# Attention and two MoE layers on one core: the first weight splits pinned behind exponentials, an early activation, and the first weight loads queued behind rows of q and k

## The chip, the cores and the metric

One core of one Trainium2 chip runs the whole kernel. The metric is the time of one execution on the device in microseconds (us), as the median of several runs.

## What is computed

Random-feature attention over 4 batches, 8 heads, 576 positions of 64 elements, and then two feed-forward layers over its 2304 rows of 512. The weights of both layers come in float64; everything else is float32.

```python
def phi(x):                                  # q and k, both scaled by 64 ** -0.25
    h = x @ omega.T - sum(x * x) / 2         # 128 features
    return exp(h - max(h)) / sqrt(128)
kv, z = k_p.T @ v, sum(k_p)                  # per head
attn = (q_p @ kv) / (q_p @ z + 1e-6)
x = attn.transpose(0, 2, 1, 3).reshape(2304, 512)
x = ((x @ w_a) * (x @ w_b)) @ w_out          # d_ff 1536: 12 slabs f of 128
out = relu(x @ w_in) ** 2 @ w_out2           # d_ff 2048: 16 slabs
```

## The kernel before

Matmuls of the two layers run as three products of a high and a low part, so each float64 weight slab is loaded raw as pairs of 32-bit words and split on chip: `load` (L125) issues the DMAs on SP into one of two raw buffers, `split` (L142) makes the two parts with three ScalarE instructions (L151, L152, L163) and five of VectorE (L155, L159, L164, L168, L172). `load_split` (L184) does the load at once and puts the split on a list; `step()` (L196), called once for each step of the work around it, counts the list down, and a split is written into the program three steps after its load. The split tiles `a` and `p` exist once, so splits run one after the other.

The program is given as a sequence; a scheduler then orders the instructions of each engine by their place in it and by when it expects their inputs, and adds the semaphores. An engine runs its own list in order.

At the start, `prologue` (L233) transposes `omega` on TensorE and makes `OMS`, `OMZ` and `OM` of it on ScalarE (L247 to L251). `start_lanes` (L805) then does batch 0: `k_lane(0, (0,))`, and for each pair of heads p the steps of q, merged in turns with those of the next k pair. A k pair (`k_steps`, L407) loads its rows (`Side`, L310) and V, transposes them (`t1_main`, L330), copies them to `S` (L333), projects and exponentiates in two halves (`phi_wide`, L278: matmuls L285, a minimum L289, four exponentials L291), and multiplies with V (L423). A q pair (`q_steps`, L463) does the same for its rows up to the exponentials, transposes the features (L474), multiplies (L481), divides and turns the result into `x_all` (L492 to L499). The sequence makes 54 steps, 0 to 53: k pair 0 with its tail 0 to 9, q pair 0 with k pair 1 10 to 20, q pair 1 with k pair 2 21 to 36, q pair 2 with k pair 3 37 to 47, q pair 3 48 to 53. The exponentials of k pair 0 stand at steps 4 and 6, of k pair 1 at 15 and 17, of k pair 2 at 30 and 33; rows of q pair 0 and k pair 1 are loaded at 10 and 11, of q pair 1 and k pair 2 at 21 and 22.

Between those steps the loop at L887 takes the first weights from `get_first` (L873): the first slabs of `w_a` and `w_b` (key `("a", 0)`), then `w_out`'s first (`("o", 0)`), and so on, one call of it at each step S0, S0 + SD, and so on. With S0 = 1, SD = 8 the loads stand at steps 1, 17, 25, 41 and 49. After the lanes the MoE passes begin (`a_units`, L599): `proj` (L610) multiplies x with `w_a` and `w_b`, `outs` (L635) with `w_out`, and the rest of attention runs in their gaps.

Of the kernel before, what the change touches and what calls it, by code (L numbers as in the profile page):

```python
# [8 lines left out]
F32 = mybir.dt.float32  # L9
# [4 lines left out]
ACTF = mybir.ActivationFunctionType  # L14
# [21 lines left out]
def f32(ap):  # L36
    return ap.bitcast(F32)


def i32(ap):  # L40
    return ap.bitcast(I32)
# [3 lines left out]
def kernel(  # L45
# [13 lines left out]
    nc = tc.nc  # L59
# [65 lines left out]
    def load(*parts):  # L125


        raw = top["raw"].tile([128, 2, 512, 2], I32, tag="raw", name="raw")
        for x, (w, f, rows) in enumerate(parts):
            t = raw[:, x]  # L130
            if rows:
                nc.sync.dma_start(
                    out=t.rearrange("p f w -> p (f w)"), in_=w[f * 128:(f + 1) * 128, :]
                )
            else:
                nc.sync.dma_start(
                    out=t.rearrange("p (k f) w -> p k (f w)", k=KC),
                    in_=w[:, f * 256:(f + 1) * 256].rearrange("(k p) f -> p k f", p=128),
                )
        return raw[:, 0:len(parts)]  # L140

    def split(raw, t):  # L142

        n = raw.shape[1]
        up = raw[:, :, :, 1]
        u = raw[:, :, :, 0]
        a = top["cut"].tile([128, 2, 512], F32, tag="a", name="a")[:, 0:n]
        p = top["cut"].tile([128, 2, 512], F32, tag="p", name="p")[:, 0:n]  # L150
        nc.scalar.activation(out=a, in_=f32(up), func=ACTF.Copy, scale=WORD_SCALE)  # L151
        nc.scalar.activation(  # L152
            out=u, in_=raw.bitcast(U16)[:, :, :, 1], func=ACTF.Copy, scale=2.0 ** 7,
        )
        nc.vector.tensor_scalar(  # L155
            out=i32(p), in0=i32(a), scalar1=3, scalar2=0x7FFFF000,
            op0=ALU.logical_shift_left, op1=ALU.bitwise_and,
        )
        nc.vector.scalar_tensor_tensor(  # L159
            out=i32(p), in0=i32(a), scalar=-0x80000000, in1=i32(p),  # L160
            op0=ALU.bitwise_and, op1=ALU.bitwise_or,
        )
        nc.scalar.copy(out=t[:, :, 0, :], in_=p)  # L163
        nc.vector.scalar_tensor_tensor(  # L164
            out=u.bitcast(U32), in0=up.bitcast(U32), scalar=23, in1=u.bitcast(U32),
            op0=ALU.logical_shift_left, op1=ALU.bitwise_or,
        )
        nc.vector.tensor_scalar(  # L168
            out=i32(a), in0=i32(p), scalar1=-0x00800000, scalar2=None,
            op0=ALU.bitwise_and,  # L170
        )
        nc.vector.scalar_tensor_tensor(  # L172
            out=t[:, :, 1, :], in0=u.bitcast(U32), scalar=2.0 ** -43, in1=a,
            op0=ALU.mult, op1=ALU.mult,
        )
# [4 lines left out]
    def split_next():  # L180
        _, _, fn = waiting.pop(0)
        fn()

    def load_split(key, parts, t, steps, then=None):  # L184
        while len(waiting) > 1:
            split_next()
        raw = load(*parts)

        def fn():
            split(raw, t)  # L190
            if then:
                then()

        waiting.append([steps, key, fn])
# [11 lines left out]
    def get_pair(key, steps, pool, tag, *parts):  # L206
        t = pool.tile([128, 2, 2, 512], F32R, tag=tag, name=tag)
        load_split(key, parts, t, steps)
        return t[:, 0], t[:, 1]
# [4 lines left out]
    ap2 = actx.enter_context(tc.tile_pool(name="ap2", bufs=2))  # L214
# [11 lines left out]
    state = {"at": [0, 1, 2, 3, 4, 5, 6, 7], "n": 0}  # L226

    def at_bank(shape, name):
        i = state["at"][state["n"] % len(state["at"])]
        state["n"] += 1  # L230
        return bank(i, shape, name)

    def prologue():  # L233
        make_identity(nc, ident)
        nc.sync.dma_start(out=om[:, 0, :], in_=omega)
        nc.sync.dma_start(out=om[:, 1, :], in_=omega)


        nc.vector.memset(V, 1.0)
        nc.vector.memset(VT, 1.0)  # L240
        nc.vector.memset(VT[64:128, :, :, 0, :], 0.0)
        nc.vector.memset(VT[0:64, :, :, 1, :], 0.0)
        nc.vector.memset(OMZ, 0.0)
        ps = at_bank([128, M], "ps_om")
        nc.tensor.transpose(ps, om.rearrange("p a d -> p (a d)"), ident)

        nc.scalar.mul(out=OMS, in_=ps, mul=-SCALE)  # L247
        for x in range(2):
            r = slice(64 * x, 64 * x + 64)
            nc.scalar.mul(out=OMZ[r, x, :], in_=ps[r], mul=-SCALE)  # L250
        nc.scalar.copy(out=OM[:, 0, :], in_=OMS)  # L251
        nc.vector.tensor_tensor(out=OM[:, 1, :], in0=OMS, in1=f32(OM[:, 0, :]), op=ALU.subtract)
# [25 lines left out]
    def phi_wide(rows, dst):  # L278


        n = 2 * len(rows)
        nm = ap2.tile([128, n], F32, tag="nm", name="nm", bufs=4)
        ps = at_bank([128, n, M], "ps_p")
        for x, s in enumerate(rows):
            nc.tensor.matmul(  # L285
                ps[:, 2 * x:2 * x + 2].rearrange("p h m -> p (h m)"), lhsT=s,
                rhs=OMZ.rearrange("p h m -> p (h m)"), start=True, stop=True,
            )
        nc.vector.tensor_reduce(out=nm, in_=ps, axis=AXX, op=ALU.min)  # L289
        for x in range(n):  # L290
            nc.scalar.activation(  # L291
                out=dst[:, x, :], in_=ps[:, x, :], func=ACTF.Exp, scale=-1.0,
                bias=nm[:, x:x + 1],
            )

    class Side:
# [4 lines left out]
        def __init__(self, src, nm, b, p, chunks):  # L301
            self.nm = nm
            self.wide = (nm, b) in WIDE or (nm, b) == ("q", 1) and 0 in chunks
            self.main = chunks
            nj = len(chunks)
            h = slice(2 * p, 2 * p + 2)
            j0 = chunks[0]
            self.nat = ap1.tile([128, 2, nj, D], F32, tag=f"{nm}n", name=f"{nm}n", bufs=2)
            v_ = src[b, h, 0:SM, :].rearrange("h (p j) d -> p h (j d)", j=4)
            nc.sync.dma_start(  # L310
                out=self.nat.rearrange("p h j d -> p h (j d)"),
                in_=v_[:, :, j0 * D:(j0 + nj) * D],
            )
# [59 lines left out]
    def kt_steps(b, g):  # L373
# [13 lines left out]
        yield  # L387
        kp = ap2.tile([128, 2, M], F32, tag="qp", name="kpt", bufs=2)
        phi_wide([st], kp)
        yield  # L390

# [409 lines left out]


    prologue()

    def start_lanes():  # L805
# [67 lines left out]
    def get_first():  # L873
        for f in range(W_FIRST):
            get_w(f)
            yield
            yield
            get_wo(f)
            yield
        for f in range(W_FIRST, 3):  # L880
            get_wo(f)
            yield

    lanes, n = start_lanes()
    first = get_first()
    S0, SD = 1, 8
    for i, _ in enumerate(lanes):  # L887
        step()
        if i >= S0 and (i - S0) % SD == 0:
# [105 lines left out]
```

## Time and profile before

| | us |
|---|---|
| median of 3 runs | 1050.73 |
| lowest and highest | 1049.35, 1052.2 |
| the profiled execution | 1052.61 |
| its span, first to last instruction | 1050.8 |
| TensorE busy in the span | 1024.0 |

The profile is of one execution. Its rows give for each engine when it worked, how long it was idle and what ended the idle time. PE is TensorE's matmuls, PEld its weight loads, which run beside them; ACT is ScalarE, DVE VectorE, POOL GpSimd, SP the engine that issues most DMAs. Ends of matmuls are modelled, so a busy PE isn't PE at its peak.

### The profile page before, as it was taken

How to read it: one execution, taken by the hardware profiler on the slowest of the kernel's cores; microseconds unless marked ns; L12 is line 12 of the kernel's file. 1: busy time of each engine (PE TensorE's matmuls, PEld its weight loads, DVE VectorE, ACT ScalarE, POOL GpSimd, SP SyncE). 2: the span in 40 equal slices, each digit the busy share in tenths (PEclk: the TensorE clock that was granted, in tenths of full speed). 3: DMA queues.
4: the chain of work that ended last, by engine and by line, in shares of the span. 5: the costliest groups of instructions: out<-in, count | busy, mean ns of one | idle time of the engine just before them, and what ended most of it. 6: DMA issues, size and time to landing. Idle time of an engine off the chain costs nothing.

```text
span 1050.8 us, 14948 instructions
## 1 busy us (share of the span) xinstructions
PE 1024.0 (97%) x5641; PEld 873.6 (83%) x5641; DVE 526.8 (50%) x1274; ACT 471.2 (45%) x1079; POOL 28.9 (3%) x54
## 2 busy tenths in 40 slices
PE   4899999999999999999999999999999999999998
PEld 3789989999988877788888888788788888888887
DVE  4788885665654445444337987722222322322222
ACT  4887757554455443333326665522322322322232
POOL 3100101000000000000000000000000000000000
PEclk9999999999999999999999999999999999999999
DMA  6846864663432211312227664300200200100010
GB/s 166 242 148 205 267 233 120 210 209 95 142 105 80 63 46 56 95 62 70 66 87 264 230 220 174 107 1 0 81 1 1 71 1 1 51 1 1 0 41 21
DMA packets 83144, 105.90 MB, mean 101 GB/s; under 512 B 26240, under 2 KB 65152, under 8 KB 83072
## 3 DMA queue, kind: packets, MB, share of 16 engines
q1 hardware_dynamic: 81536, 103.37, 30.7%
q0 software_dynamic: 1536, 1.58, 0.5%
q8 instruction: 45, 0.74, 0.3%
q14 instruction: 27, 0.22, 0.1%
HBM read 87.62 MB, written 17.30 MB: 100 GB/s over the span
## 4 chain that ended last, share of the span: by engine, by line
PE 88%; DVE 4%; DMA 3%; ACT 3%; issue 1%; SPq 1%; ACTq 0%; DVEq 0%
PE abw L610 19%; PE o L764 19%; PE ph L777 18%; PE y L635 12%; PE ab L610 7%; PE ps_n L481 3%; PE ps_p L285 2%; PE ps_kv L423 2%; PE ps_p L351 2%; PE ps_qt L474 1%; DMA raw<-in_moe_w_out_dram 1%; PE ps_t L330 1%; DMA qn<-in_q_dram 1%; DVE p L159 1%; PE ps_x L492 1%
## 5 line engine op out<-in xcount | busy, mean ns | idle before, releaser
L635 PE MATMUL y<-gs,wo 128*128 128x256 f32 (+1 forms) x864 | 177.2, 345 | 0.0
L764 PE MATMUL o<-w,ss 128*128 128x512 f32 x702 | 170.9, 390 | 1.4 <-ACT ss L786 1.4
L777 PE MATMUL ph<-yx,w 128*128 128x512 f32 (+1 forms) x780 | 169.8, 368 | 0.0
L777 PEld LDWEIGHTS ph<-yx,w 128*128 128x128 f32 x780 | 137.4, 188 | 25.3
L785 DVE TENSOR_TENSOR r<-r 128x512 f32<-128x512 f32 (+1 forms) x80 | 51.1, 639 | 209.8 <-ACT r L784 209.8
L764 PEld LDWEIGHTS o<-w,ss 128*128 128x128 f32 x702 | 130.5, 188 | 29.7 <-ACT ss L786 2.2
L635 PEld LDWEIGHTS y<-gs,wo 128*128 128x128 f32 x864 | 136.6, 190 | 15.2
L610 PE MATMUL abw<-x_all,w 128*128 128x512 f32 x576 | 146.6, 398 | 0.0
L784 ACT ACTIVATE r<-ph 128x512 f32<-128x512 f32 (+1 forms) x80 | 44.5, 556 | 208.4 <-PE ph L777 208.2
L610 PE MATMUL ab<-x_all,w 128*128 128x256 f32 x864 | 132.9, 295 | 0.3 <-DVE x_all L549 0.2
L610 PEld LDWEIGHTS abw<-x_all,w 128*128 128x128 f32 x576 | 105.5, 189 | 19.2
L610 PEld LDWEIGHTS ab<-x_all,w 128*128 128x128 f32 x864 | 115.0, 193 | 1.5 <-DVE x_all L549 0.5
L787 DVE TENSOR_TENSOR ss<-r,ss 128x512 fp32r<-128x512 f32 (+1 forms) x80 | 51.1, 639 | 46.6 <-ACT ss L786 40.0
L610 PE MATMUL abw<-x_mid,w 128*128 128x512 f32 x288 | 73.1, 400 | 0.0
L786 ACT CAST ss<-r 128x512 fp32r<-128x512 f32 (+1 forms) x80 | 46.2, 577 | 51.5 <-DVE r L785 51.5
L610 PEld LDWEIGHTS abw<-x_mid,w 128*128 128x128 f32 x288 | 52.1, 189 | 9.8
L358 DVE CUSTOM_DVE_ANT_0 c<-ps_p,c 128x128 f32<-128x128 f32 x152 | 37.8, 287 | 32.5 <-ACT c L356 32.0
L701 ACT CAST gs<-a_s 128x256 fp32r<-128x256 f32 (+1 forms) x96 | 40.6, 433 | 28.3 <-DVE a_s L700 28.1
L164 DVE SCALAR_TENSOR_TENSOR raw<-raw 128x1024 uint32<-128x1024 uint32 (+1 forms) x40 | 42.5, 1062 | 13.4 <-ACT raw L152 13.3
L152 ACT ACTIVATE raw<-raw 128x1024 int32<-128x1024 uint16 (+1 forms) x40 | 40.8, 1020 | 11.4 <-DMA raw<-in_moe_w_out_dram 9.3
L702 DVE TENSOR_TENSOR gs<-a_s,gs 128x256 fp32r<-128x256 f32 (+1 forms) x96 | 42.8, 454 | 5.3 <-ACT gs L701 4.2
L151 ACT ACTIVATE a<-raw 128x1024 f32<-128x1024 f32 (+1 forms) x40 | 40.6, 1014 | 10.9 <-DMA raw<-in_moe_w_out_dram 5.6
(109 smaller groups left out, 1212.9 us busy)
## 6 DMA issues: line engine op xcount, KB each, us to landing
wo<-wo_d SPq DMA_DIRECT2D x60, 512.0 KB, 3.5
raw<-in_moe_w_out_dram SPq DMA_DIRECT2D x28, 512.0 KB, 4.8
raw<-in_moe_w_in_dram SPq DMA_DIRECT2D x16, 512.0 KB, 3.9
raw<-in_moe_w_a_dram SPq DMA_DIRECT2D x12, 512.0 KB, 4.8
raw<-in_moe_w_b_dram SPq DMA_DIRECT2D x12, 512.0 KB, 6.1
wo_d<-wo SPq DMA_DIRECT2D x12, 512.0 KB, 3.4
kn<-in_k_dram SPq DMA_DIRECT2D x16, 256.0 KB, 3.5
V<-in_v_dram SPq DMA_DIRECT2D x16, 256.0 KB, 3.4
```

Source lines behind the costliest of these rows:

```text
L151: nc.scalar.activation(out=a, in_=f32(up), func=ACTF.Copy, scale=WORD_SCALE)
L152: nc.scalar.activation(out=u, in_=raw.bitcast(U16)[:, :, :, 1], func=ACTF.Copy, scale=2.0 ** 7,)
L164: nc.vector.scalar_tensor_tensor(out=u.bitcast(U32), in0=up.bitcast(U32), scalar=23, in1=u.bitcast(U32), op0=ALU.logical_shift_left, op1=A ...
L610: nc.tensor.matmul(ps, lhsT=wv[:, s_, kc, :], rhs=x[..., kc, m_, :], start=(kc == 0 and (s_, m_) == TERMS[0]), stop=(kc == KC - 1 and (s_, ...
L635: nc.tensor.matmul(y_part(pi, f, c), lhsT=wo[pi, f][:, s_, c * 128:(c + 1) * 128], rhs=g[:, m_, :],  start=(f == f0 and (wide or c % 2 == ...
L702: nc.vector.tensor_tensor(out=g[:, 1, c], in0=a_s, in1=f32(g[:, 0, c]), op=ALU.subtract)
L764: nc.tensor.matmul(op[t], lhsT=s_t[f][:, s_, t * 128:(t + 1) * 128], rhs=wo2[f][:, m_, :], start=(f == 0 and (s_, m_) == TERMS[0]), stop=( ...
L777: nc.tensor.matmul(ps, lhsT=wv[:, s_, kc, :], rhs=y[:, kc, m_, :], start=(kc == 0 and (s_, m_) == TERMS[0]), stop=(kc == KC - 1 and (s_, m ...
L784: nc.scalar.activation(out=r, in_=ps, func=ACTF.Relu, scale=1.0 / W_SCALE)
L785: nc.vector.tensor_tensor(out=r, in0=r, in1=r, op=ALU.mult)
L786: nc.scalar.copy(out=s_t[f][:, 0, :], in_=r)
L787: nc.vector.tensor_tensor(out=s_t[f][:, 1, :], in0=r, in1=f32(s_t[f][:, 0, :]), op=ALU.subtract)
```

## The change

An Exp of a column of zeros is put at the head of the prologue. `Side` and `phi_wide` record the last row load and the last exponential that they have written. For the keys `("a", 0)` and `("o", 0)` the raw load is queued, on SP, behind the row load recorded last, and the split's ScalarE instructions behind the exponential recorded last: `issue_after` orders what the block writes on that instruction's own engine behind it. S0 becomes 16 and SD 6, which puts the loads at steps 16, 28, 34, 46 and 52.

```diff
-        raw = load(*parts)
+        if key in (("a", 0), ("o", 0)):
+            with tc.issue_after(state["row"].ins):
+                raw = load(*parts)
+        else:
+            raw = load(*parts)
 
         def fn():
-            split(raw, t)
+            if key in (("a", 0), ("o", 0)):
+                with tc.issue_after(state["exp"].ins):
+                    split(raw, t)
+            else:
+                split(raw, t)
...
     def prologue():
+        warm = ap2.tile([128, 1], F32, tag="den", name="warm", bufs=3)
+        nc.vector.memset(warm, 0.0)
+        nc.scalar.activation(out=warm, in_=warm, func=ACTF.Exp)
         make_identity(nc, ident)
...
         for x in range(n):
-            nc.scalar.activation(
+            state["exp"] = nc.scalar.activation(
                 out=dst[:, x, :], in_=ps[:, x, :], func=ACTF.Exp, scale=-1.0,
...
-            nc.sync.dma_start(
+            state["row"] = nc.sync.dma_start(
                 out=self.nat.rearrange("p h j d -> p h (j d)"),
...
-    S0, SD = 1, 8
+    S0, SD = 16, 6
```

## Rows read from the trace of the kernel before

**Rows 1.** The page, first part: busy us (share of the span) and instructions.

```profile
PE 1024.0 (97%) x5641; PEld 873.6 (83%) x5641; DVE 526.8 (50%) x1274; ACT 471.2 (45%) x1079; POOL 28.9 (3%) x54
```

**Rows 2.** Stages: length, busy PE, PEld, DVE, ACT, POOL, granted clock, DMA share, GB/s.

```profile
0.00:15.00 15.00, 1.86 (x7) 1.20 (x8) 2.50 (x6) 3.10 (x6) 7.79 (x18) 1.00 0.80 218
15.00:25.00 10.00, 9.76 (x48) 8.20 (x49) 7.81 (x12) 8.38 (x24) 0.00 (x0) 1.00 0.34 96
25.00:60.00 35.00, 30.66 (x207) 26.01 (x206) 28.59 (x56) 31.74 (x87) 4.72 (x8) 1.00 0.75 227
60.00:140.00 80.00, 79.78 (x611) 75.55 (x611) 68.70 (x147) 59.74 (x143) 9.41 (x16) 1.00 0.67 211
```

**Rows 3.** Waits, 0 to 62 us: us in total, times, longest.

```profile
PE ps_t L330 <- ACT OMZ L250: 8.7, 1, 8.7
ACT a L151 <- DMA raw<-in_moe_w_b_dram: 1.3, 1, 1.3
```

**Rows 4.** Timeline, 0 to 30 us: start, us, engine, line, operation.

```profile
3.22 0.45 PE L245 MATMUL ps_om<-ident,om 128*128 128x128 f32 x1 [3.22 <-DMA om<-in_omega_dram]
4.90 1.11 PE L330 MATMUL ps_t<-ident,kn 128*128 128x128 f32 x4 [1.24 <-DMA kn<-in_k_dram]
...
11.85 1.28 ACT L151 ACT_TABLE_LOAD   x1 [11.85 <-DMA raw<-in_moe_w_b_dram]
13.14 1.12 ACT L151 ACTIVATE a<-raw 128x1024 f32<-128x1024 f32 x1
14.16 0.27 ACT L247 ACTIVATE OMS<-ps_om 128x128 f32<-128x128 f32 x1
...
15.21 0.59 ACT L333 COPY S<-ps_t 128x512 f32<-128x512 f32 x1
...
26.95 1.22 ACT L291 ACTIVATE kp<-ps_p,nm 128x128 f32<-128x128 f32 x4
```

**Rows 5.** SP's issues (timeline), and DMA issues of 0 to 5 us: median to landing.

```profile
4.27 0.50 SPq L310 DMA_DIRECT2D qn<-in_q_dram  x1
4.82 0.92 SPq L310 DMA_DIRECT2D kn<-in_k_dram  x1
...
qn<-in_q_dram SPq DMA_DIRECT2D x1, 128.0 KB, 8.7
kn<-in_k_dram SPq DMA_DIRECT2D x1, 256.0 KB, 9.3
...
kn<-in_k_dram SPq DMA_DIRECT2D x1, 256.0 KB, 3.2
V<-in_v_dram SPq DMA_DIRECT2D x1, 256.0 KB, 4.8
```

**Rows 6.** Groups of ScalarE, 0 to 30 us: busy us, mean ns, idle before.

```profile
L152 ACT ACTIVATE raw<-raw 128x1024 int32<-128x1024 uint16 (+1 forms) x2 | 1.8, 920 | 0.0
L151 ACT ACTIVATE a<-raw 128x1024 f32<-128x1024 f32 (+1 forms) x2 | 1.8, 909 | 0.0
L163 ACT CAST w<-p 128x1024 fp32r<-128x1024 f32 x1 | 1.1, 1050 | 0.0
L163 ACT CAST wo<-p 128x512 fp32r<-128x512 f32 x1 | 0.7, 719 | 0.0
```

**Rows 7.** Last split steps (timeline), and L610's matmuls in two stretches.

```profile
20.30 1.22 DVE L172 SCALAR_TENSOR_TENSOR w<-raw,a 128x1024 fp32r<-128x1024 uint32 x1
67.20 1.23 DVE L172 SCALAR_TENSOR_TENSOR w<-raw,a 128x1024 fp32r<-128x1024 uint32 x1
...
46.00:68.00 22.00, 9.10 (x56) 1.00 0.76 230
68.00:70.00 2.00, 2.00 (x18) 1.00 0.26 60
```

**Rows 8.** Groups of PE, forms apart, 0 to 20 us, then 20 to 26.

```profile
L285 PE MATMUL ps_p<-OMZ,S 128*128 128x256 f32 x8 | 3.8, 651 | 0.2 <-ACT S L333 0.2
...
L285 PE MATMUL ps_p<-OMZ,S 128*128 128x256 f32 x12 | 3.7, 393 | 0.0
```

## The prediction

> **What bounds the kernel now.** I read the page's busy totals first [rows 1]: TensorE is busy 1024.0 of 1050.8 us, so no edit here can save more than the 26.8 us in which it is idle, and only where the idle time lies matters. The stages [rows 2] say where: from 0 to 15 us PE is busy 1.86 us (13.1 idle), from 15 to 60 us 40.42 of 45 (4.6 idle) and from 60 to 140 us 79.78 of 80. The change touches the beginning alone, so the question is what ends the waits there. The waits name it: the longest one of PE, 8.7 us, is the transpose of q behind `OMZ` [rows 3]. The rows in order of time [rows 4] show why `OMZ` is late. Omega's transpose ends at 3.22 + 0.45 = 3.67 us, and the transposes of the first k pair start at 4.90 and end near 6.0. But ScalarE's first instruction is the first weight split (L151), which waits until 11.85 us for `w_b`; its table load (1.28 us) and its own 1.12 us follow, and `OMS` and `OMZ`, ready to run at 3.67, stand behind it until 14.16 us. The k slab's copy `S` follows at 15.21 us. One instruction issued too early on an in-order engine holds attention back by some 10 us.
>
> There is a second wait under the first. q's first rows are issued at 4.27 us behind both halves of the first weights and land 8.7 us later, at 13.0; the second k pair's, issued at 4.82, land at 14.1 [rows 5]. PE has the transposes of q ahead of the projections of k, so with ScalarE free alone PE would have stood until 13.0 anyway. The two edits need each other.
>
> **The change part by part.** *The early activation* adds a memset of one column, an Exp of one column and moves the table load ahead. The table load was 1.28 us behind the DMA wait, inside the stall, so it isn't added to the gain of the stall. The one-column Exp isn't in the trace; its bound above is a 128x128 one, 1.22 us for four, so 0.3, and the memset's is the same 0.3. Both and the table load are done when they start by 3.67 - 1.28 - 0.6 = 1.8 us, before ScalarE has its first real work, and nothing but the memset stands before them. Counted at nothing; without that cover they would cost up to 1.9.
>
> *The pin of the splits.* I count steps in the lane loop. S0 = 16 loads the first weights at step 16 and, three steps on, traces their split at step 19; the exponentials recorded last by then are the second half of k pair 1 (step 17), the second pair and not the first. w_out's first split is loaded at step 28, traced at 31, pinned behind the first half of k pair 2 (step 30). In the trace of before the k pair 1 exponentials end at 26.95 + 1.22 = 28.2 us [rows 4]. ScalarE is therefore free at 3.67: `OMS`, `OMZ`, `OM` (1.05 us, from 14.16 to `S` at 15.21) run until 4.7, and `S` can start when the k transposes end, at 6.05 instead of 15.21: 9.15 us earlier.
>
> *The loads behind the rows.* SP issues the two weight halves behind q's first rows and k pair 1's, so these take the issue slots at 2.9 and 3.4 us. What they then need is bounded by the nearest rows: k pair 0, issued into an empty queue, 3.2 us, and V, issued just behind it, 4.8 us [rows 5]. So q lands between 6.1 and 7.7 and k pair 1 between 6.6 and 8.2. I take q at 6.8: PE then projects k from about 7.2 instead of 15.85, and the gain on this chain is 8.6 us, between 8.1 and 9.15. The weights themselves land some 1.3 us later than at 11.85, hidden, since their split waits for 19.6 (28.2 - 8.6). w_out's load is put behind the rows of k pair 2, which can't be issued before the first k buffer is read, near 6.2; its split is due near 28, hidden by more than 10 us. POOL's small loads (tails of k, q and v) are not moved past anything; they share the DMA engines.
>
> *Where the stall goes.* The splits of the first weights and of the first w_out cost ScalarE 1.8 + 1.8 + 1.1 + 0.7 = 5.4 us [rows 6], and until now they lay in 13 to 29 us, mostly in gaps of the first k pair's chain. Now they come behind it, in a stage in which ScalarE has little room: it is busy 31.74 of 35 us from 25 to 60, 91% [rows 2]. This is what is late next. Up to 25 us the chain comes 8.6 us earlier (16.4). From there to the point that was 60 us, ScalarE has the 31.74 us and the part of the splits that had lain before 25 us, 5.4 - 0.7 = 4.7: 36.4 us. With no idle time at all it is done at 16.4 + 36.4 = 52.8 (gain 7.2); at the 91% it kept, 36.4 / 0.907 = 40.1, at 56.5 (gain 3.5). I take 95%, the middle, since part of its 3.3 us idle was a wait for a weight load that now has more time: 38.3, at 54.7, **a gain of 5.3 us**. From 60 us on PE is full and the rest moves up unchanged, wherever the weights keep up.
>
> *S0 and SD* as such put the five early splits at steps 19, 31, 37, 49 and 55 instead of 4, 20, 28, 44 and 52: the later ones move little. There are two raw buffers, so each later load waits for an earlier split. That is costed under the rivals.
>
> The profiled execution took 1052.61 us with a span of 1050.8 us (1.8 lie around the span). It would become 1052.6 - 5.3 = 1047.3; it lies 1.9 us above the median of the runs shown, 1050.73, so the median becomes **1045.4**.
>
> **The rivals.**
> *A, all of the stall comes back:* the extra splits find room in ScalarE's gaps, and PE fills its own with MoE work. For it: from 25 to 60 PE waits for many small things, and its weight-load row is busy only 26.01 of 35 us [rows 2]. Against: 99% would be asked of ScalarE. Gain 8.6 to 9.1: 1041.9.
>
> *B, given back to the weights:* the fourth weights are used from the 73rd matmul of L610 on, since the first three make 24 each. 56 have started by 68.0 and 18 more by 70.0, so this is at about 69.9 us; the fourth split's last step ends at 67.20 + 1.23 = 68.4 us [rows 7]. The slack is 1.5 us. If attention comes 5 to 9 us earlier and the splits don't, PE has to fill with other work or wait here. VectorE, which does most of a split, is busy 68.70 of 80 us from 60 to 140 [rows 2], 86%. Against: PE was kept full there by reordered work. A gain of 0 to 3.4 is left, middle 1.7: 1049.0.
>
> *C, slower:* the split loop doesn't compress. The first split starts at 19.6 instead of 13.1, 6.5 us later, and frees its raw buffer as much later; through two buffers this would go on to each later weight. The fourth weights would come at 68.4 + 6.5 = 74.9, and PE, which used them at 69.9, loses 5.0: 1055.7. It decides from the point at which the fourth split ends after 69.9. Against: the buffers stood unused between 21.5 us (first split's last step, 20.30 + 1.22) and the next use, and ScalarE even waited for the next weights' load [rows 7, 3].
>
> *D, it doesn't do what it says:* the order that is pinned doesn't free `OMZ`, or q's rows land as late as before because the engines serve the queue's transfers together. The waits then still end near 13; gain 0 to 1, 1050.2.
>
> *E, matmuls stay slow for longer:* the first eight projections of k took 651 ns each in the mean before 20 us, the next twelve 393 ns, while the granted clock reads 1.00, the level of 2.4 GHz, in both [rows 8, 2]. PE had stood for 8.7 us before the slow ones. If a start with gaps keeps the slow pace through q's and k pair 1's projections, too, 12 matmuls cost 0.26 more in duration; since durations overlap, the bound is 12 x 0.26 = 3.1 and the pace (3.8 us for eight against 3.7 for twelve) gives 12 x 0.17 = 2.0. I take 2.0: gain 3.3, 1047.4. The Trainium skill, "TensorE: Matmul & The Clock Gate", Part 1, says that the engine starts at half its clock and that activity releases it: a kernel that begins earlier with sparse work would by this stay slow until the work is dense. The slow durations agree with it; the granted clock's row here doesn't show it.
>
> **How the numbers follow.** Forecast (gain 3.5 to 7.2, 1043.5 to 1047.2) 0.48; A 0.17; B 0.15; C 0.08; D 0.06; E 0.06. Predicted is 1045.4. The range takes in A, at 1041.0 with q landing early (8.1 to 9.15 and some of PE's small gaps), and most of B and D: 1041.0 to 1050.5; outside stay C, half of D and the ends of A, about 0.15. A measurement of this kernel can tell about 0.3%, 3.15 us, from no change, so faster means under 1047.6: forecast, A, half of E and a fifth of B, 0.71. Same is the rest of B and E, and D, 0.21. Slower is C, 0.08.
>
> **What would show it.** The table load over before 3.67 us; `OMZ` before 5; PE's 8.7 us wait gone, and its busy time from 0 to 15 us up from 1.9 to about 9; q's first rows landing before 8. L151 first behind the eight exponentials of k pair 1, near 20 us. ScalarE's share over 93% in the stage that follows, and PE's idle time there above the 4.6 us of before by about 3. The first L610 matmul about 5 us earlier than now. I am wrong low if that stage gives PE no new idle time; wrong high if PE waits for w or wo between 55 and 100 us.

## The result, and the profile after

| | before | after |
|---|---|---|
| median (us), lowest to highest | 1051.44, 1049.35 to 1052.27 | 1057.54, 1054.23 to 1061.95 |
| the profiled execution, its span | 1052.61, 1050.8 | 1056.90, 1055.1 |
| TensorE busy, idle in the span | 1024.0, 26.8 | 1026.3, 28.8 |

The ratio after to before is 1.0061, with a 95% interval of 1.0038 to 1.0085: slower by some 6 us, where 1045.4 us and a gain of 5.3 had been predicted.

The start of the changed kernel, its timeline (start, us, engine, line, operation, in brackets the idle time before and what ended it). L341, L344, L296 and L302 are the lines L330, L333, L285 and L291 of before:

```profile
0.74 1.28 ACT L244 ACT_TABLE_LOAD   x1 [0.74 <-PEq L987]
2.03 0.20 ACT L244 ACTIVATE warm<-warm 128x1 f32<-128x1 f32 x1
3.70 0.28 ACT L258 ACTIVATE OMS<-ps_om 128x128 f32<-128x128 f32 x1 [1.47 <-PE ps_om L256]
...
6.07 0.59 ACT L344 COPY S<-ps_t 128x512 f32<-128x512 f32 x1 [1.33 <-PE ps_t L341]
...
7.62 0.66 PE L341 MATMUL ps_t<-ident,qn 128*128 128x128 f32 x2 [1.59 <-DMA qn<-in_q_dram]
8.07 1.06 PE L296 MATMUL ps_p<-OMZ,S 128*128 128x256 f32 x2
...
18.40 1.19 ACT L302 ACTIVATE kp<-ps_p,nm 128x128 f32<-128x128 f32 x4
19.42 1.19 ACT L151 ACTIVATE a<-raw 128x1024 f32<-128x1024 f32 x1
```

All of this is as forecast: `S` at 6.07 instead of 15.21, the first projection at 8.07 instead of 15.85, the first split right behind k pair 1's exponentials at 19.42 [rows 4, 8]. By 25 us PE had started 104 matmuls instead of 55.

The stages, with the columns of [rows 2], show where that went:

```profile
0.00:15.00 15.00, 8.94 (x47) 7.39 (x47) 4.22 (x11) 7.20 (x21) 7.78 (x18) 1.00 0.85 236
15.00:25.00 10.00, 8.61 (x57) 7.40 (x57) 6.16 (x12) 8.48 (x21) 3.55 (x6) 1.00 0.50 128
25.00:60.00 35.00, 28.51 (x182) 24.10 (x180) 26.55 (x51) 27.38 (x74) 1.17 (x2) 0.95 0.67 210
60.00:140.00 80.00, 74.32 (x547) 69.07 (x546) 63.54 (x133) 55.32 (x132) 7.20 (x12) 0.98 0.57 180
```

PE's idle time (length less busy) falls by 7.1 us up to 15 us and grows by 1.2, 2.2 and 5.5 us in the next three stages [rows 2]. Its lead of 49 matmuls at 25 us is 24 at 60 us and a lag of 43 at 140 us (counted by stages, the last one in two halves; a matmul that runs across a border counts on both sides). The granted clock adds to it, 0.95 and 0.98 where before it was 1.00. The waits of PE from 15 to 100 us (us in total, times, longest) and the rows around the two longest:

```profile
PE ps_p L296 <- ACT S L344: 4.1, 3, 2.9
PE ab L621 <- ACT w L163: 2.5, 1, 2.5
PE ps_qt L485 <- ACT qp L302: 2.2, 1, 2.2
```

```profile
34.67 1.12 ACT L152 ACTIVATE raw<-raw 128x1024 int32<-128x1024 uint16 x1
35.69 1.16 ACT L151 ACTIVATE a<-raw 128x1024 f32<-128x1024 f32 x1
36.73 0.59 ACT L344 COPY S<-ps_t 128x512 f32<-128x512 f32 x1
37.37 1.69 PE L296 MATMUL ps_p<-OMZ,S 128*128 128x256 f32 x4 [2.91 <-ACT S L344]
...
68.97 1.23 DVE L159 SCALAR_TENSOR_TENSOR p<-a,p 128x1024 int32<-128x1024 int32 x1
71.67 1.22 DVE L172 SCALAR_TENSOR_TENSOR w<-raw,a 128x1024 fp32r<-128x1024 uint32 x1
72.93 1.14 ACT L152 ACTIVATE raw<-raw 128x1024 int32<-128x1024 uint16 x1 [2.53 <-DMA raw<-in_moe_w_b_dram]
73.93 1.06 ACT L163 CAST w<-p 128x1024 fp32r<-128x1024 f32 x1
...
75.05 0.99 PE L621 MATMUL ab<-x_all,w 128*128 128x256 f32 x4 [2.46 <-ACT w L163]
```

At 37.37 PE waits for a copy that stands on ScalarE behind two instructions of a split; at 75.05 (L621 is L610 of before) it waits for the high part of the fourth weights, which the cast L163 makes. That isn't a wait for their load: what the cast reads was ready at 70.20 (L159's end), and the fourth split's last step (L172) ends at 72.89. But on ScalarE the cast stands behind L152 of the fifth slab, and that one waits for the fifth slab's load, which landed at 72.93. After both, the clock falls (stages of 2.5 us, same columns):

```profile
37.50:40.00 2.50, 2.50 (x9) 2.09 (x10) 2.27 (x4) 0.89 (x5) 0.00 (x0) 0.56 0.96 331
40.00:42.50 2.50, 2.50 (x16) 2.19 (x15) 1.37 (x3) 2.50 (x7) 0.00 (x0) 0.76 0.10 39
75.00:77.50 2.50, 2.45 (x9) 2.13 (x9) 0.66 (x2) 1.81 (x3) 0.00 (x0) 0.57 0.40 157
77.50:80.00 2.50, 2.50 (x18) 2.39 (x16) 1.51 (x4) 0.90 (x4) 0.00 (x0) 0.75 0.00 0
```

### The profile page after: what moved, and what is told of

Same layout as the page of the kernel before. It is cut to its first block, busy times and chain, and to the rows that moved or that the text cites. A ratio compares the mean times of both kernels' runs of the same rounds, so it can differ in the third digit from the quotient of the medians.

```text
span 1055.1 us, 14946 instructions
## 1 busy us (share of the span) xinstructions
PE 1026.3 (97%) x5641; PEld 874.4 (83%) x5641; DVE 527.8 (50%) x1275; ACT 473.0 (45%) x1080; POOL 29.0 (3%) x54
## 5 line engine op out<-in xcount | busy, mean ns | idle before, releaser
L621 PE MATMUL abw<-x_all,w 128*128 128x512 f32 x576 | 146.6, 398 | 0.0
L621 PE MATMUL ab<-x_all,w 128*128 128x256 f32 x864 | 132.1, 294 | 3.3 <-ACT w L163 2.5
L621 PEld LDWEIGHTS abw<-x_all,w 128*128 128x128 f32 x576 | 105.5, 189 | 19.3
L621 PEld LDWEIGHTS ab<-x_all,w 128*128 128x128 f32 x864 | 114.7, 192 | 5.4 <-ACT w L163 2.7
L621 PE MATMUL abw<-x_mid,w 128*128 128x512 f32 x288 | 73.0, 399 | 0.0
L621 PEld LDWEIGHTS abw<-x_mid,w 128*128 128x128 f32 x288 | 52.1, 189 | 9.8
L712 ACT CAST gs<-a_s 128x256 fp32r<-128x256 f32 (+1 forms) x96 | 40.6, 433 | 27.1 <-DVE a_s L711 26.8
L152 ACT ACTIVATE raw<-raw 128x1024 int32<-128x1024 uint16 (+1 forms) x40 | 40.7, 1016 | 16.6 <-DMA raw<-in_moe_w_out_dram 10.5
L151 ACT ACTIVATE a<-raw 128x1024 f32<-128x1024 f32 (+1 forms) x40 | 40.5, 1012 | 9.2 <-DMA raw<-in_moe_w_out_dram 6.9
```

Of the source, the lines that this page charges most:

```text
L152: nc.scalar.activation(out=u, in_=raw.bitcast(U16)[:, :, :, 1], func=ACTF.Copy, scale=2.0 ** 7,)
L621: nc.tensor.matmul(ps, lhsT=wv[:, s_, kc, :], rhs=x[..., kc, m_, :], start=(kc == 0 and (s_, m_) == TERMS[0]), stop=(kc == KC - 1 and (s_, ...
L712: nc.scalar.copy(out=g[:, 0, c], in_=a_s)
```

## The experiments

Ratios are to the kernel before on the same chip, with 95% intervals; "4th" and "8th" are the ends of the fourth split of a w_a/w_b slab and of the eighth split of all (timeline of L172, start plus duration), "idle" is PE's from 25 to 60 us, "lead" its matmuls started by 140 us less the 876 of before.

| | ratio | 4th | 8th | idle | lead |
|---|---|---|---|---|---|
| before | 1 | 68.4 | 77.0 | 4.3 | 0 |
| after | 1.0061 [1.0038, 1.0085] | 72.9 | 85.1 | 6.5 | -43 |
| e1_steps_only | 1.0033 [1.0018, 1.0048] | 75.5 | 84.6 | 2.1 | -18 |
| e2_pins_only | 0.9998 [0.9986, 1.0011] | 73.8 | 83.2 | 5.0 | -48 |
| e3_later_loads_as_before | 1.0022 [1.0009, 1.0035] | 78.0 | 87.0 | 5.0 | -29 |
| e4_every_4_steps | 1.0024 [1.0014, 1.0035] | 78.6 | 87.9 | 3.7 | -4 |
| e5_first_split_early | 1.0010 [0.9994, 1.0027] | 71.2 | 80.5 | 6.1 | -25 |
| e6_first_early_every_6 | 1.0064 [1.0039, 1.0089] | 71.9 | 83.9 | 4.7 | -29 |
| e7_no_first_loads | 0.9957 [0.9942, 0.9972] | 61.6 | 70.1 | 2.8 | +51 |
| e8_activation_only | 0.9993 [0.9978, 1.0007] | | | 4.0 | |
| e9_steps_one_later | 1.0059 [1.0038, 1.0080] | 72.3 | 79.5 | 2.8 | -14 |
| e10_a_pinned_order_kept | 1.0002 [0.9990, 1.0013] | 68.3 | 76.9 | 4.1 | -9 |
| e11_early_weights_and_rows | 0.9947 [0.9930, 0.9964] | 68.8 | 78.2 | 1.7 | +4 |
| e12_rows_behind_weights | 1.0000 [0.9986, 1.0014] | 71.9 | 81.2 | 1.6 | -15 |
| e13_early_first_rest_late | 0.9983 [0.9969, 0.9996] | 69.8 | 78.9 | 1.7 | +29 |
| e14_steps_one_later_early | 0.9951 [0.9937, 0.9966] | 65.8 | 75.2 | 1.8 | +23 |
| e15_first_behind_both_halves | 0.9972 [0.9960, 0.9985] | 66.9 | 76.2 | 3.7 | +23 |
| e16_one_later_behind_both | 0.9981 [0.9966, 0.9996] | 68.5 | 80.3 | 2.9 | -19 |

The last two columns don't give the time by themselves: matmuls differ in length, an engine at a low clock is busy and not idle, and some time is still won or lost after 140 us (e13 below).

**Parts alone.** e1_steps_only is the kernel before with the new steps and nothing else:

```diff
-    S0, SD = 1, 8
+    S0, SD = 16, 6
```

> The kernel before with only S0 = 16, SD = 6; no pin, no early activation. Theory W (weights late: the first loads and splits are written 4 to 15 steps later, two raw buffers pass this on, and from 60 us on TensorE waits for weights): the fourth slab's split ends near 73 us as in the changed kernel (72.9) and not at 68.4, TensorE's idle time from 60 to 140 us is 3 to 6 us, time 1053 to 1058. Rival P (it is the pins, which put three ScalarE instructions of a split in a row ahead of work that TensorE waits for): without pins the idle time from 25 to 60 us falls from 6.5 to 4 or less, time 1045 to 1050.

It takes 1056.12 us. The late loads free the start a little (PE idle 7.8 us to 15 us), yet more than half of the change's loss is there without a single pin. Its price isn't waiting: over the whole span PE is idle for 22.0 us, 4.8 less than before, but busy for 1032.1, 8.1 more with as many matmuls. From 15 to 25 us it works at the low clock (columns of [rows 2]), behind a wait of 2.41 us at 15.41:

```profile
15.00:25.00 10.00, 9.59 (x34) 8.45 (x35) 5.27 (x8) 6.30 (x22) 1.17 (x2) 0.53 0.23 62
```

e2_pins_only is the changed kernel with the old steps:

```diff
-    S0, SD = 16, 6
+    S0, SD = 1, 8
```

> The changed kernel with S0 = 1, SD = 8 as before: pins and early activation alone. The first split is now pinned behind the first half of k pair 0's exponentials and its load behind k pair 0's rows, so q's rows still land near 13 us. Theory W: weights come as early as before or earlier (fourth split ends at 68 or before), no wait for weights from 60 us on (idle under 1 us from 60 to 140), the gain is what the first stage gives with q at 13: 1 to 4 us, 1047 to 1050. Rival P: pins cost in the stage from 25 to 60 us, idle there 6 us or more, 1052 to 1056.

1052.24 us, no change. The first weights go ahead of q's rows again, and PE waits for these until 13.09 us: the second wait under the first that the prediction had read from [rows 5] is real.

e8_activation_only adds the early Exp alone to the kernel before.

> The kernel before with the early activation alone; the order of all engines stays (5284 of 5288 on TensorE). The table load of 1.28 us moves out of the stall, the wait for the weights and for q's rows (13 us) stays. Theory O: 1.0 to 1.3 us faster than before, ratio 0.9988. Rival R: no change, ratio 1.000.

1051.91 us, its interval holds both theories; the 1.1 us that q's transposes come earlier (13.77 for 14.91) can't be told from nothing.

**The steps of the loads, with the change's pins.** e3 keeps the changed kernel's first load at step 16 and puts the others back to 18, 25, 41, 49; e4 takes every fourth step from 16; e5 loads the first slab at 11, splits it one step later and has the others at 17, 25, 41, 49; e6 does the same first and then takes every sixth step.

```diff
-        if i >= S0 and (i - S0) % SD == 0:
+        if i in AT:      # e3: (16, 17, 18, 25, 33, 41, 49); e5: (11, 13, 17, 25, 33, 41, 49)
...
-    S0, SD = 16, 6
+    S0, SD = 16, 4       # e4;  e6: 11, 6
...
+get_pair(("a", f), 3 if f else 1, ...   # e5, e6
```

> The changed kernel with the first weights still loaded at step 16, but the other early loads at steps 18 (w_out's first), 25, 41 and 49, as before (17, 25, 41, 49), instead of 28, 34, 46 and 52. Theory W: the second slab's split ends before 38 us (43.4 in the changed kernel), the fourth's before 68.4, TensorE's wait of 2.5 us for w near 75 us is gone, idle time from 60 to 140 us under 2 us (5.7 in the changed kernel), time 1044 to 1049. Rival S (ScalarE is simply too full in the stage from 16 to 60 us, whatever the order of the weights): the idle time from 25 to 60 us stays at 6 us or more and takes the gain, 1051 to 1056.

> The changed kernel with SD = 4: loads at steps 16, 24, 28, 36 and 40. Theory W: like the run before it, weights a little later for the first and earlier for the later ones; idle time from 60 to 140 us under 2 us, 1044 to 1050. Rival S: more splits in the full stage, idle time from 25 to 60 us 7 us or more, 1053 to 1059.

> The changed kernel with the first weights loaded at step 11 (still behind q's and k pair 1's rows on SP) and their split written one step later, at 12, so that it is pinned behind the exponentials of k pair 0 and its tail and not of k pair 1; the other early loads at steps 17, 25, 41 and 49, as before. Theory W2 (the first split decides: in the changed kernel and in all variants so far it ended at 25.6 to 28.9 us against 21.5 before, and freed the first of two raw buffers so much later; each later slab followed 3 to 9 us late): the first split ends near 20, the second slab's near 34, the fourth's near 66, no wait of TensorE for w, and the 8 us of the start are kept for the most part: 1044 to 1048. Rival C2 (pauses of TensorE between 20 and 60 us, each followed by microseconds at half clock, take the gain whatever the weights do): the granted clock from 25 to 60 us is 0.9 or less and the time 1050 to 1055.

> The same early first split, with S0 = 11 and SD = 6 for the rest: loads at steps 11, 23, 29, 41 and 47. Theory W2: w_out's first slab is 6 steps later than in the run before, so the second buffer is freed late; the time lies between that run and the changed kernel, 1046 to 1052. Rival C2: no order between these two beyond what the clock of the stage from 25 to 60 us gives; 1050 to 1056.

1055.35, 1055.34, 1053.64 and 1058.14 us. Putting the later loads back is worth 0.0039 from the changed kernel to e3 and 0.0054 from e6 to e5, 4 and 6 us. It isn't that weights come sooner: e3's fourth split ends 5 us after that of the changed kernel. Like e1, e3 and e4 pay in busy time (1029.3 and 1030.7 us in the span, 1024.0 before) and not in idle time (25.4 and 22.9, 26.8 before). And e5 has its first five splits as early as before (22.6 to 48.7 us; before 21.5 to 49.5), its start 7 us ahead, and still gains nothing.

**Is it the order?** Any of these edits makes the scheduler write all engines in another order: counted from the two programs, 5008 of TensorE's 5288 instructions and 907 of ScalarE's 1082 stand in the changed kernel in the sequence of before. e7 keeps the sequence (5218 and 1028) and takes away what stalls the start:

```diff
-        raw = load(*parts)
+        if key in (("a", 0), ("o", 0)):
+            raw = top["raw"].tile([128, 2, 512, 2], I32, tag="raw", name="raw")[:, 0:len(parts)]
+            nc.vector.memset(raw, 0)
+        else:
+            raw = load(*parts)
```

> The kernel before, in which the raw tiles of the first w_a/w_b slab and of the first w_out slab are set to zero by VectorE and not loaded: these three loads are left out, so the result lacks those slabs; all other work is there and nearly all instructions of each engine stand in the order of before (5218 of 5288 on TensorE, 1028 of 1082 on ScalarE). No split waits for a DMA at the start, and q's rows have no weights ahead of them. Theory O (the order decides: before's order of the engines would keep what the start gives, and the changed orders lose it in in-order waits; here the weights are also early, first split done before 12 us): TensorE's 8.7 us wait is gone, idle time from 60 to 140 us stays under 1 us, 1042 to 1046. Rival R (the stage from 15 to 160 us can't run faster, whatever the order, since its chains of ScalarE, VectorE and transfers set it): the idle time comes back between 15 and 160 us, 1048 to 1053.

e9 moves every first load of the kernel before one step on, with no gain at the start (4976 and 949 in sequence):

```diff
-    S0, SD = 1, 8
+    S0, SD = 2, 8
```

> The kernel before with S0 = 2 and not 1: every early load is written one step later; nothing at the start can gain from this. The scheduler gives another order after it (4976 of 5288 on TensorE stand as before, 949 of 1082 on ScalarE). Theory O: an order that was not chosen loses 2 to 6 us against before with idle time of TensorE of 3 us or more between 60 and 160 us: 1053 to 1057. Rival R: as before, 1050.5 to 1052.5.

1047.93 and 1059.24 us. e7 leaves out the loads of three slabs, so it is no kernel to use; it keeps at the end what it gains at the start: with the sequence kept, every split is 5.5 to 10 us earlier, to the last one. e9 loses as much as the whole change by one step of the loads. Most of its price stands in two waits, each followed by a stretch at a granted clock of 0.5 to 0.8:

```profile
PE ps_xt L542 <- DVE xh L459: 4.1, 1, 4.1
PE ps_kv L423 <- ACT kp L291: 2.0, 1, 2.0
```

So I held for a time that a new order as such costs 6 us or more, which the next pair was to test.

**A real version of both.** e10 and e11 have the old steps, the early Exp, and q pair 0's and k pair 1's rows loaded ahead of the first weights. e10 queues the first w_a/w_b split alone behind the first half of k pair 0's exponentials, which happens to keep the sequence (5267 and 1072); e11 queues w_out's first split behind the same one, which doesn't (4821 and 913). In e10 the pin is written with `state["exp"]`, which is the same instruction at that step.

```diff
     def get_first():
+        pre["q", 0, 0] = Side(q, "q", 0, 0, [0, 1])
+        pre["k", 0, 1] = Side(k, "k", 0, 1, (0, 1, 2, 3))
...
         def fn():
-            split(raw, t)
+            if key in (("a", 0), ("o", 0)):        # e10: key == ("a", 0)
+                state.setdefault("exp0", state["exp"])
+                with tc.issue_after(state["exp0"].ins):
+                    split(raw, t)
```

> Steps of the loads as before (1, 9, 17, ...), early Exp, the rows of q pair 0 and k pair 1 loaded ahead of the first weights, and only the split of the first w_a/w_b slab queued behind k pair 0's first exponentials. 5267 of TensorE's 5288 instructions and 1072 of ScalarE's 1082 stand in the order of before. On ScalarE one instruction of w_out's first split still stands ahead of the first exponentials and waits for its load, which landed at 15.7 us in before, so these exponentials should come near 16.3 us (18.7 before) and the start should gain 2 to 3 us. Theory O (what the start gains is kept where the order of the engines is kept): ratio 0.9975, 1049 us. Rival R (whatever the start gains is given back before 160 us): ratio 1.000 or above.

> As the run beside it, but both first splits (w_a/w_b's and w_out's) queued behind k pair 0's first exponentials, so that nothing at the start waits for weights: first exponentials near 10 us, first weights as early as in before or earlier, 8 us gained at 15 us. The order of the engines after that is another (4821 of TensorE's 5288 in the order of before, 913 of ScalarE's 1082). Theory W (the changed kernel lost its gain because its weights came late): weights early here, gain kept, ratio 0.9925, 1044 us. Theory O (the new order loses 6 to 12 us in waits and half-clock stretches between 25 and 160 us, whatever the weights do): ratio 0.998 to 1.004, 1050 to 1056 us.

e10 keeps the order and gains nothing; e11 takes a new order and is the fastest kernel so far, 1047.84 us, 5.6 us under before. The theory that the order alone decides falls. ScalarE's timeline says what sets the two apart; e10 first, then e11:

```profile
15.34 0.65 ACT L152 ACTIVATE raw<-raw 128x512 int32<-128x512 uint16 x1 [5.83 <-DMA raw<-in_moe_w_out_dram]
15.90 1.13 ACT L303 ACTIVATE kp<-ps_p,nm 128x128 f32<-128x128 f32 x4
```

```profile
10.58 1.14 ACT L303 ACTIVATE kp<-ps_p,nm 128x128 f32<-128x128 f32 x4 [1.31 <-DVE nm L301]
13.20 1.12 ACT L151 ACTIVATE a<-raw 128x1024 f32<-128x1024 f32 x1 [1.48 <-DMA raw<-in_moe_w_b_dram]
14.22 1.13 ACT L152 ACTIVATE raw<-raw 128x1024 int32<-128x1024 uint16 x1
15.23 1.14 ACT L303 ACTIVATE kp<-ps_p,nm 128x128 f32<-128x128 f32 x4
```

In e10 one instruction of w_out's split, which was not pinned, holds the exponentials for 5.83 us. Its first w_a/w_b split ends 4 us later than before, its second at the same 29.1 us, and every later one within 1.2 us of before. From there all runs as before, and the lead of PE at 15 us (18 matmuls for 7) is gone by 25. In e11 the first half of the exponentials waits for no weights, and the first split lies between the halves, ahead of q's work and of k pair 1's; the second half stands behind its two instructions, the first of which waits 1.48 us for w_b. PE's idle time from 25 to 60 us is 1.7 us, at a granted clock of 0.90.

**The order held, the start moved.** e12 is e11 without the early rows; TensorE, ScalarE and VectorE keep exactly e11's sequence, and only two loads move on SP.

```diff
     def get_first():
-        pre["q", 0, 0] = Side(q, "q", 0, 0, [0, 1])
-        pre["k", 0, 1] = Side(k, "k", 0, 1, (0, 1, 2, 3))
```

> e11_early_weights_and_rows without its early loads of q pair 0's and k pair 1's rows: these stand on SP behind the first weights again. TensorE, ScalarE and VectorE keep exactly the order of e11; only two loads move on SP. Theory Q (the place of the rows on SP carries the gain of e11): q's rows land near 13 us (7.2 in e11), ScalarE's copy of them stands ahead of the first exponentials and holds them up until then, the first split ends some 4 us later, ratio 0.999. Theory O (e11's order of the engines carries it): a loss at the start is taken up by the time x is ready, ratio 0.995.

1051.0 us, 0.0053 over e11: q's transposes start at 12.34 instead of 7.24 us. The last steps of four splits, e11 first, then e12:

```profile
18.64 1.21 DVE L172 SCALAR_TENSOR_TENSOR w<-raw,a 128x1024 fp32r<-128x1024 uint32 x1
27.07 0.68 DVE L172 SCALAR_TENSOR_TENSOR wo<-raw,a 128x512 fp32r<-128x512 uint32 x1
...
58.85 1.21 DVE L172 SCALAR_TENSOR_TENSOR w<-raw,a 128x1024 fp32r<-128x1024 uint32 x1
67.56 1.23 DVE L172 SCALAR_TENSOR_TENSOR w<-raw,a 128x1024 fp32r<-128x1024 uint32 x1
```

```profile
22.81 1.22 DVE L172 SCALAR_TENSOR_TENSOR w<-raw,a 128x1024 fp32r<-128x1024 uint32 x1
30.25 0.68 DVE L172 SCALAR_TENSOR_TENSOR wo<-raw,a 128x512 fp32r<-128x512 uint32 x1
...
62.00 1.21 DVE L172 SCALAR_TENSOR_TENSOR w<-raw,a 128x1024 fp32r<-128x1024 uint32 x1
70.72 1.22 DVE L172 SCALAR_TENSOR_TENSOR w<-raw,a 128x1024 fp32r<-128x1024 uint32 x1
```

The distance is 4.2 us at the first and 3.1 to 3.2 at the others, and it is still 2.9 at the seventeenth (157.1 and 160.0). Nothing compresses here: theory Q, against O. In e10 it did: its first split is 3.9 us later than before and the second on time. In the kernel before, SP had issued the second half of the next w_a/w_b load only at 24.81, behind a load of V; in e10 it did so at 25.94, so 1.1 us were left of the 3.9.

e13 is e11 with the changed kernel's steps for all loads but the first, e14 is e11 with all of them one step on.

```diff
-    S0, SD = 1, 8
+    AT = (1, 22, 28, 34, 40, 46, 52)   # e13
+    S0, SD = 2, 8                      # e14
```

> e11_early_weights_and_rows with its first load at step 1 as there and the other first loads at the steps of the changed kernel (28, 34, 46, 52 in the place of 17, 25, 41, 49). The start up to 15 us is that of e11. Theory W (late loads of the later slabs are what costs): the splits from the second slab on end some 6 us or more later than in e11 and TensorE waits for w again before 100 us, ratio 1.000 to 1.003. Theory F (only the first slab's lateness counts, since it holds up the others over the two raw buffers): these splits end at most 2 us later, ratio 0.995.

> e11_early_weights_and_rows with each first load one step later (2, 18, 26, 42, 50), as e9 did to the kernel before. 5149 of TensorE's 5288 instructions and 1033 of ScalarE's 1083 keep the order of e11. Theory W (early loads and a start that waits for nothing carry the gain): ratio 0.995 to 0.996. Theory O (any new order costs 5 us or more, and e11's was a lucky one): ratio 1.000 or above, with new waits or half-clock stretches between 60 and 160 us.

1050.36 and 1046.97 us. e14 is as good as e11, with another order: the gain isn't that of one lucky order. e13 falls between its two theories, 0.0036 over e11, though its fourth and eighth splits end within 1.1 us of e11's; so F is right that the later weights don't come later, and W that the steps cost something. W's wait for w shows once, 1.29 us at 90.96. Where e13 falls back is later: at 140 us it is 25 matmuls ahead of e11, and from 140 to 200 us PE is idle for 3.8 us, in e11 for 1.6 (columns of [rows 2], e11 first); the longest waits there are for VectorE and ScalarE in the work on the pairs, not for weights:

```profile
140.00:200.00 60.00, 58.40 (x478) 57.11 (x478) 44.58 (x123) 40.92 (x98) 6.14 (x11) 1.00 0.63 198
140.00:200.00 60.00, 56.18 (x449) 54.89 (x450) 44.42 (x118) 40.77 (x96) 4.66 (x8) 0.97 0.60 193
```

Last, e15 is e11 and e16 is e14 with the first split behind both halves of k pair 0's exponentials instead of between them.

```diff
-    get_pair(("a", f), 3, wpool, ...
+    get_pair(("a", f), 3 if f else 6, wpool, ...   # e15;  e16: 5
```

> e11_early_weights_and_rows with one change: the first w_a/w_b split is queued behind both halves of k pair 0's exponentials instead of between them (its list count is 6 steps instead of 3). 5232 of TensorE's 5288 instructions and 1044 of ScalarE's 1083 keep the order of e11; loads stand at the same steps. Theory G (e11 gains because the first split fills a wait of ScalarE between the two halves): the split then lies beside q's work as in e5, ends near 21 to 22 us (19.9 in e11), TensorE idles 4 us or more from 25 to 60 us (1.7 in e11), ratio 1.000. Theory P (it only has to stand ahead of k pair 1's exponentials): idle there stays under 2.5 us, ratio 0.995 to 0.996.

> The same change made to e14_steps_one_later_early (steps 2, 18, 26, 42, 50): first split behind both halves, list count 5. 4966 of TensorE's 5288 instructions keep e14's order. Theory G: TensorE idles 4 us or more from 25 to 60 us, ratio 1.000. Theory P: ratio 0.995 to 0.996. If this and the run beside it come out apart by over 0.4%, the order behind the start decides more than the place of the first split.

1049.21 and 1049.96 us: 0.0025 and 0.0030 over e11 and e14, some 3 us. Neither theory has the size; the place between the halves is worth about half of what G asked for.

**What they add up to.** Four kernels, all with the early Exp and the rows ahead of the weights, make a table of two places by two sets of steps:

| first splits pinned | later loads as before | every sixth step from 16 |
|---|---|---|
| behind the first half of k pair 0's exponentials | e11: 0.9947 | e13: 0.9983 |
| behind k pair 1's exponentials and later ones | e3: 1.0022 | after: 1.0061 |

The place costs 0.0075 and 0.0078, 7.9 and 8.2 us; the steps cost 0.0036 and 0.0039, 3.8 and 4.1 us. Each is the same at either level of the other as far as can be told: with intervals of 0.0013 to 0.0024 on each entry, a difference is known to 0.002 to 0.003. Together they make the 12 us between e11 and the changed kernel. e11, with the start freed, is 5.6 us under before; 12 less 5.6 is the loss seen.

The end of the first split parts the kernels, e8 and e9 left out, whose starts hardly change: in those that gain (e7, e11, e13 to e16) it comes between 11.95 and 21.46 us, in those that don't (after, e1 to e6, e10, e12) between 22.15 and 28.90; before has 21.52. It doesn't give the size: e6 has it 4.8 us earlier than the changed kernel, with the early loads at every sixth step, too, and the same time (1.0064 and 1.0061).

## Why the prediction was wrong, point by point

**What bounds the kernel: right.** The wait for `OMZ` and the wait for q's rows under it were the stall. e2, e10 and e12 each leave one hold on the chain and gain nothing.

**The activation and the start: right.** The forecast had `S` at 6.05 (6.07 measured), the projections near 7.2 (8.07), the first split at 19.6 (19.42); 7.8 us were gained in the place of 8.6.

**ScalarE as the next bound: the step failed.** ScalarE was to work 95% of the stage from 16.4 to 54.7 us. It worked 29.26 of these 38.3 us, 76%, and from 25 to 60 us 27.38 of 35, less than before (31.74). What a split costs there isn't its 5.4 us of ScalarE but the places it takes in a sequence: at 36.73 a copy that PE needs stands behind L152 and L151, while ScalarE had stood idle for 1.04 and 1.35 us before its instructions at 25.86 and 27.58. PE's idle time from 15 to 60 us did grow by 3.3 us, about the 3 forecast, but by such waits and not by a full engine. The first MoE matmul of L621 starts at 45.1 us (46.5 before), not 5 us earlier: most of attention's lead was gone by then. The place of the first splits costs 8 us by the table above, and the forecast had charged 3.3 for it.

**"The later ones move little": the step failed.** Moving the later loads by up to 11 steps was counted at nothing; it costs 3.8, 4.1 and 5.7 us in the three pairs e11 to e13, e3 to after and e5 to e6. How it does so isn't shown. Weights that come late are a small part at most: e13's come no later than e11's, and it and e3 wait for w once each up to 140 us, 1.29 us. A poorer sequence of the pairs' work and the splits is the reading that e9 and e13's waits behind 140 us speak for, but that was only argued.

**"The rest moves up unchanged" from 60 us on: the step failed.** PE idled 5.7 us from 60 to 140 us where before it idled 0.2. The longest wait is that for the fourth weights at 75.05. They weren't due at 69.9 us: of the 18 matmuls that the forecast added to 56, two were running at 68.0 and counted among the 56, and the kernel before starts its 73rd at 73.26, 4.8 us after the fourth split and not 1.5. Rival C had 74.9 for these weights and 1055.7 us for the time; it got 0.08. Its chain can be seen in the rows: a load is issued when the split that used its buffer ends. The changed kernel's first split ends 5.4 us later than before and its third 5.2 (64.19 + 1.21 = 65.40 us, 60.23 before); SP's issues for the fifth slab follow at once, and w_b lands at 72.93:

```profile
65.59 0.37 SPq L136 DMA_DIRECT2D raw<-in_moe_w_a_dram  x1
66.01 0.50 SPq L136 DMA_DIRECT2D raw<-in_moe_w_b_dram  x1
```

But that C's 74.9 was met is in part luck. The fourth split itself ended at 72.89, 4.5 us late. The rest came from ScalarE's order: with its input ready at 70.20, the fourth slab's cast stood behind the fifth's L152 and so waited for the late load. In the kernel before it stands ahead of it:

```profile
65.99 1.05 ACT L163 CAST w<-p 128x1024 fp32r<-128x1024 f32 x1
...
67.21 1.18 ACT L152 ACTIVATE raw<-raw 128x1024 int32<-128x1024 uint16 x1
...
73.26 0.75 PE L610 MATMUL ab<-x_all,w 128*128 128x256 f32 x5
```

This is the fault that the change was to remove, moved by 60 us: an instruction that waits for a load stands ahead of one that is ready.

The evidence against C was misread. That "the buffers stood unused between 21.5 us" and the next use rested on the end of the first split alone. One more view of the kernel before, SP's issues beside the ends of the splits, would have told otherwise: the first split ends at 20.30 + 1.22 = 21.52 us [rows 7], and the fifth slab's load is issued at 60.29, right behind the third slab's split, which ends at 59.00 + 1.23:

```profile
21.57 0.37 SPq L136 DMA_DIRECT2D raw<-in_moe_w_a_dram  x1
...
60.29 0.37 SPq L136 DMA_DIRECT2D raw<-in_moe_w_a_dram  x1
```

So the buffers weren't free, and a late first split can be passed on from split to split. e12 shows this with every engine's order but SP's kept, 4.2 us at the first split and 3 at each one after, though its late rows of q hold up the pairs' work, too. e10 shows the limit: 3.9 us at the first split and none at the second. Whether two buffers are too few stays open: a third one doesn't fit beside what the kernel holds, and no run has one.

**Rival E, the clock: wrong place, but a part of the loss.** Slow matmuls didn't stay on from the start: the first eight projections took 544 ns in the mean, those after 11 us 392. But the clock fell later, for 10 us in all at a mean granted clock of 0.66 in the four rows shown; that is 3.4 us of TensorE's work at the full clock, an upper estimate of its price. In the whole span PE is busy for 2.3 us more than before, with as many matmuls, about half of the 4.3 us by which the span grew; E had charged 2.0 us. The Trainium skill, "TensorE: Matmul & The Clock Gate", Part 1, says that TensorE goes back to half its clock after idling. The rows at 37.5 and 75.0 us agree: each follows a wait of 2.91 or 2.46 us.

**What stays open.** e5 and e15 have the first split in the same place, the same steps from the second load on and their first five splits within 1 to 3 us of each other, and differ by 0.0038. They differ in at least one more thing: w_out's first split is pinned behind the same exponential as the first in e15, behind later ones in e5, and no run moves that pin alone. Nor is it known why e6's earlier first split gains nothing on the changed kernel. e9 differs from before by one step and loses 6 us. No run here takes these apart from the sequence that the scheduler wrote, so of any single variant some 4 to 6 us can't be foretold from its edit; the two effects above rest on showing in two pairs each, of different sequences.

## What to carry to other kernels

Before work is moved behind a stall, find the chain that starts with it: here the splits, two buffers deep, and time won by attention was kept, whole or in part, only where the first split ended no later than before (e7, e11, e13 to e16). A deferred instruction cost more here by the places that it took in an in-order engine's list than by its share of that engine's time; put it where that engine waits, as e11 does between two halves of exponentials. When a wait ends with an instruction of a busy engine, look at what stands ahead of that instruction before the data it reads is called late. And where a scheduler writes the order, test a step constant by its neighbours, too, before a change of half a per cent is put down to a mechanism.

## What was not expected of the hardware

The granted clock fell after waits of 2.5 to 4 us in the middle of the work, and two or three stages of 2.5 us in a row show it low while TensorE was busy nearly all the time; e10, behind a wait of 4.03 us at 16.30:

```profile
15.00:17.50 2.50, 1.20 (x6) 1.20 (x7) 1.47 (x3) 2.16 (x6) 0.00 (x0) 0.54 0.12 36
17.50:20.00 2.50, 2.50 (x12) 2.22 (x11) 0.85 (x2) 2.50 (x7) 0.00 (x0) 0.50 0.01 2
20.00:22.50 2.50, 2.50 (x14) 2.35 (x12) 1.95 (x3) 0.97 (x5) 0.00 (x0) 0.59 0.30 103
```

0.50 is the 1.2 GHz level of the two. The length of a single wait doesn't tell: behind one of 2.23 us at 28.00 in the changed kernel the clock stayed at 1.00, behind one of 1.29 us at 90.96 in e13 it fell to 0.66. The wait of 8.7 us at the start of the kernel before did not show in it: its granted clock reads 1.00 from 0 to 25 us [rows 2], though the same matmul took 651 ns in the mean up to 20 us and 393 behind it [rows 8]. The row doesn't tell the pace of the first microseconds; the durations do.
